# Part of one weight tile loaded through Pool's queue, in loads of uneven row counts

## The chip, the core and the metric

The kernel runs on one core of a Trainium2 chip. The core has a matrix engine (PE), a vector engine (DVE), a scalar engine (ACT), Pool (GpSimd) and the sync engine (SP), and 16 DMA engines that carry all transfers between HBM and the on-chip memory of 128 partitions. SP, ACT and Pool can each issue transfers, on a queue of their own; all queues run on the same 16 DMA engines. The metric is the device time of one execution in microseconds; smaller is better.

## The reference

One decoding step of a transformer block for 8 sequences, model width 512, in float32:

```python
mod = (silu(c) @ w_mod).reshape(8, 6, 1, 512)       # sa, ca, ga, sb, cb, gb
h = layernorm(x) * (1 + ca) + sa
q = (h @ wq) as 32 heads of 128;  k, v = last 2048 rows of the caches, 8 heads, each used by 4 query heads
p = softmax(q k^T / sqrt(128));  x = x + ga * ((p v) @ wo)
h = layernorm(x) * (1 + cb) + sb
x = x + gb * (relu(h @ w1 + b1) ** 2 @ w2 + b2)
```

The caches are 8 x 8 x 8192 x 128; the window of 2048 rows makes 67 MB of K and 67 MB of V. The weights are wq (512 x 4096), wo (4096 x 512), w_mod (512 x 3072), w1 (512 x 1792) and w2 (1792 x 512). Every byte is read once and little is computed on it.

## The kernel before

The kernel is a stream of loads with the computation hung on it. On chip stand four "big" slots of 128 partitions x 32 KB and one "small" slot of 128 x 16 KB. The list `loads` gives the order: w_mod in two parts, wq in two halves, then K and V tiles of 4 MB in turn (a K tile is half of the batch for one head; V runs two tiles behind K), with wo tiles of 2 MB slipped in before the K tiles 4, 9 and 13 into the small slot, and at the end the last V tile in three pieces, the "tail" (the last wo rows with half of w1), the other half of w1, and w2 in five pieces. `pump()` issues loads from this list in order as long as the slot that the next one needs is free; `done(key)` frees a slot and pumps again. All of them are issued by SP (`nc.sync`), so a load that waits for its slot also holds those behind it. ACT issues only the small xc at the start and the two biases b1, b2 near the end. Pool sets a few constants at the start and clears one tile (L498) near the end.

A wo tile j holds the wo rows of heads 2j and 2j+1, read as 128 partitions x 2 halves x 2048 floats (four consecutive wo rows for each partition and half, so each half is one run of 8 KB). The user is `project_o(hk)` (L482), which multiplies the attention output of head hk with half of the tile and adds into `wo_ps`; `done(("wo", j))` follows the second half. So the second wo tile (key `("wo", 1)`, issued before K tile 9) can be loaded once `project_o(1)` has read the first one, and is used by `project_o(2)` and `project_o(3)`. The last wo rows come with the tail, into a big slot, and are used by `project_o(6)` and `project_o(7)`.

The order of work is written by hand (`tc.manual_schedule()`): the loop at L506 takes K tile s//2 in quarter steps. In each step DVE transposes K (L184), PE makes scores (L353), and PE multiplies the probabilities of earlier tiles with V (L442); the softmax of a head is spread over steps (L361 to L429), and `parts`, `gather` and `project_o` follow (L459 to L482). After the loop come the residual, the second layer norm, w1 (L605) and w2 (L624), and the output. `spin` (L560) is filler work of PE. Semaphores and waits between engines are set by the framework from what each instruction reads and writes; a load waits for what last used its destination.

How a load is cut is set by the shape of its access pattern. A 4 MB tile of 128 partitions becomes 128 packets of 32 KB, 8 on each DMA engine, and one mark of completion on each.

Of the kernel before, what the change touches and what calls it, by code (L numbers as in the profile page):

```python
# [8 lines left out]
F32 = mybir.dt.float32  # L9
# [4 lines left out]
EPS = 1e-5  # L14
BIG_SLOTS = 4
PV_LAG = 5

@with_exitstack
def tile_adaln_cached_attention_mlp(  # L20
# [14 lines left out]
    nc = tc.nc  # L35
    P = 128
    B, HKV, SK, DH = k_cache.shape
    D = wq.shape[0]
# [14 lines left out]
    consts = ctx.enter_context(tc.tile_pool(name="consts", bufs=1))  # L53
# [27 lines left out]
    }  # L81
    free = {size: list(range(len(ts))) for size, ts in slots.items()}
    held = {}
    r_kc = "(p kc) n -> p kc n"

    def size_of(key):
        return "small" if key[0] in ("wo", "w1") or key == ("mod", 1) else "big"

    def load(key):
        kind, i = key  # L90
        held[key] = free[size_of(key)].pop(0)
        t = slots[size_of(key)][held[key]]
        if kind in "KV":

            hk, c = divmod(i, 2)
            v = k_cache[4 * c : 4 * c + 4, hk] if kind == "K" else v_cache[c::2, hk]
            v = v[:, SK - W :, :].rearrange("u (p j) d -> p u (j d)", j=NJ)
            cuts = (0, big // 2, big * 3 // 4, big) if key == ("V", 2 * HKV - 1) else (0, big)
            for x, y in zip(cuts, cuts[1:]):
                nc.sync.dma_start(t[:, x:y], v[..., x:y])  # L100
            return

        def rows(o, v):
            n = v.shape[1] * v.shape[2]
            nc.sync.dma_start(t[:, o : o + n].rearrange("p (a n) -> p a n", n=v.shape[2]), v)

        def wo_rows(j):

            r = 2 * REP * DH
            return wo[j * r : (j + 1) * r, :].rearrange("(h p i) n -> p h (i n)", p=P, i=4)  # L110

        w1v = w1.rearrange(r_kc, p=P)
        if kind == "wo":
            rows(0, wo_rows(i))
        elif kind == "mod":

            v = w_mod.rearrange("(p kc) n -> p (kc n)", p=P)
            nc.sync.dma_start(t, v[:, big:] if i else v[:, :big])
        elif kind == "wq":

            nc.sync.dma_start(t, wq.rearrange("(p h a) n -> h p (a n)", p=P, h=2)[i])
        elif kind == "tail":
            for h in range(2):
                rows(h * 4 * D, wo_rows(HKV // 2 - 1)[:, h : h + 1])
            rows(big // 2, w1v[:, 0:2])
        elif kind == "w1":
            rows(0, w1v[:, 2:4])
        else:
            v = w2.rearrange("(p c) n -> p c n", p=P)
            for lo, hi in ((0, 8), (8, 10), (10, 12), (12, 13), (13, 14)):  # L130
                rows(D * lo, v[:, lo:hi])
# [14 lines left out]
    def pump():  # L146
        while at[0] < len(loads) and free[size_of(loads[at[0]])]:
            load(loads[at[0]])
            at[0] += 1
# [53 lines left out]
    lo = consts.tile([P, 1], F32, name="lo")  # L203
# [25 lines left out]
    h = work.tile([P, P], F32, name="h_sb", tag="one_h_sb", bufs=1)  # L229
# [6 lines left out]
    for k in (2, 3, 4):  # L236
        n = 1 << k
# [27 lines left out]
    for i, last in enumerate((16, 8)):  # L265
        at_ = 0
        while at_ < last:
            kc, m = divmod(16 * i + at_, 6)
            n = min(4 - m if m < 4 else 6 - m, last - at_)
# [235 lines left out]

    for s in range(N + PV_LAG + 1):  # L506
        g, i = divmod(s, C)
        q, h = divmod(s, 2)
        v = s - PV_LAG
        soft = 1 <= g <= HKV  # L510
# [160 lines left out]
```

## Time and profile before

| | |
|---|---|
| median of 3 runs | 394.42 us (394.18 to 394.96) |
| profiled execution | 394.1 us, span 392.3 us |
| granted clock of PE, mean | 0.891 |
| busy: PE, DVE, ACT, POOL | 254.9, 218.0, 46.2, 1.3 us |
| read from HBM | 164.67 MB, 420 GB/s over the span |
| DMA packets | 7829, of which 7728 on SP's queue (q1) |

Times in the profile are microseconds from the start of the span. "DMA share" is the mean busy share of the 16 DMA engines in a stretch; records can overlap a little, so it can exceed 1. q1 is SP's queue and q10 ACT's; q8 and q14 are marked "instruction": they bring in instructions of the engines (16 KB and mostly 8 KB a packet) and take their time on the same DMA engines. "PEld" is the weight load of PE.

### The profile page before, as it was taken

To read this page: it belongs to the slowest core of one execution; us is meant where nothing else is said; L and a number is where in the kernel's file an instruction comes from. 1 tells how busy PE (TensorE), PEld (TensorE's weight loads), DVE (VectorE), ACT (ScalarE), POOL (GpSimd) and SP (SyncE) were. 2 spreads that over 40 slices of the span, in tenths; PEclk is the share of its full clock that TensorE was granted. 3 is DMA by queue.
4 is the path that set the end of the run, shared out by engine and by line. 5 is a ranking of instruction groups with operands and counts; after the bars stand their busy time and mean duration, and the time that the engine had idled before them with its cause. 6 is when DMAs were issued, how large, how long until landed. Compare 5 with 4: busy or idle time off the path is not lost.

```text
span 392.3 us, 4679 instructions
## 1 busy us (share of the span) xinstructions
PE 254.9 (65%) x2006; PEld 78.9 (20%) x2006; DVE 218.0 (56%) x323; ACT 46.2 (12%) x89; POOL 1.3 (0%) x8
## 2 busy tenths in 40 slices
PE   0075768668228973797375927883775837994996
PEld 0021200112001321232021202220221211222433
DVE  1370399959056845783582817780766357845231
ACT  0120201410003100310031003000201003004010
POOL 0000000000000000000000000000000000000000
PEclk9997789998859996999699688999788969997899
DMA  8999999999999999999999999999999999999994
GB/s 329 426 435 439 441 438 428 431 426 403 451 428 428 426 431 431 433 434 430 428 423 434 434 436 434 426 431 428 404 449 428 429 432 434 429 419 416 424 428 173
DMA packets 7829, 165.04 MB, mean 421 GB/s; under 512 B 856, under 2 KB 1024, under 8 KB 1536
## 3 DMA queue, kind: packets, MB, share of 16 engines
q1 hardware_dynamic: 7728, 164.70, 98.2%
q8 instruction: 16, 0.26, 0.3%
q10 hardware_dynamic: 80, 0.04, 0.0%
q14 instruction: 5, 0.04, 0.0%
HBM read 164.67 MB, written 0.07 MB: 420 GB/s over the span
## 4 chain that ended last, share of the span: by engine, by line
DMA 69%; DVE 15%; PE 13%; issue 2%; ACT 1%; ACTq 0%; POOL 0%; DVEq 0%; POOLq 0%; SPq 0%
DMA big<-in_A_k_cache_dram 55%; DVE kT L184 9%; PE s_ps L353 7%; DMA big<-in_A_wo_dram 6%; DMA big<-in_B_w_dram 5%; DMA xc_in<-in_xc_dram 3%; PE o_ps L442 2%; PE m_ps L298 1%; DVE pT L421 1%; PE p_ps L386 1%; DVE pr L414 1%; DVE o_sb L460 1%; DVE qst L262 0%; DVE o_sb L459 0%; ACT L227 0%
## 5 line engine op out<-in xcount | busy, mean ns | idle before, releaser
L184 DVE STREAM_TRANSPOSE kT<-big 128x1024 f32<-128x1024 f32 x128 | 151.5, 1221 | 91.4 <-DMA big<-in_A_k_cache_dram 87.8
L353 PE MATMUL s_ps<-kT,qst 128*32 128x512 f32 x512 | 129.8, 1074 | 21.3 <-DVE kT L184 21.1
L442 PE MATMUL o_ps<-big,pT 128*32 128x256 f32 x1024 | 71.3, 402 | 2.6 <-DMA big<-in_A_v_cache_dram 1.6
L442 PEld LDWEIGHTS o_ps<-big,pT 128*32 128x32 f32 x1024 | 34.3, 118 | 84.7 <-issue 66.6
L369 PE MATMUL m_ps<-ident,mx 128*1 128x128 f32 x16 | 4.3, 364 | 59.9 <-DVE mx L367 59.9
L353 PEld LDWEIGHTS s_ps<-kT,qst 128*32 128x32 f32 x512 | 16.0, 117 | 40.1 <-DVE kT L184 30.7
L421 DVE STREAM_TRANSPOSE pT<-pr 128x2048 f32<-128x2048 f32 x8 | 18.2, 2275 | 1.0 <-ACT pr L404 1.0
L404 ACT ACTIVATE pr<-pr,own 128x512 f32<-128x512 f32 x16 | 17.8, 1228 | 0.3
L363 ACT COPY ss<-s_ps 128x512 f32<-128x512 f32 x8 | 4.7, 586 | 101.7 <-issue 73.2
L398 ACT ACTIVATE pr<-p_ps,nm 128x512 f32<-128x512 f32 x8 | 5.5, 688 | 94.6 <-DVE nm L395 94.6
L341 ACT COPY qst<-q_ps 32x128 f32<-32x128 f32 x32 | 8.2, 257 | 71.2 <-PE q_ps L330 70.9
L298 PE MATMUL m_ps<-big,h1T 128*32 128x512 f32 x64 | 11.6, 896 | 6.1 <-DMA big<-in_A_wq_dram 4.1
L466 PE MATMUL m_ps<-o_sb,pick 128*128 128x256 f32 x16 | 6.2, 469 | 14.4 <-DVE o_sb L460 14.4
L369 PEld LDWEIGHTS m_ps<-ident,mx 128*1 128x1 f32 x16 | 0.7, 80 | 65.1 <-DVE mx L367 65.1
L218 PE MATMUL m_ps<-xsum,sel 128*128 128x1 f32 x2 | 0.6, 363 | 18.5 <-DVE xsum L216 18.5
L316 DVE COPY qbd<-m_ps 32x128 f32<-32x128 f32 x8 | 3.0, 373 | 16.3 <-PE m_ps L313 16.2
L386 PE MATMUL p_ps<-ss,perm 128*128 128x512 f32 x16 | 11.3, 792 | 0.0
L395 DVE COPY nm<-m_ps 128x1 f32<-128x1 f32 x8 | 1.3, 159 | 17.5 <-PE m_ps L391 17.5
L414 DVE TENSOR_SCALAR pr<-pr,own 128x512 f32<-128x512 f32 x16 | 9.2, 659 | 0.8 <-ACT pr L398 0.8
L459 DVE TENSOR_SCALAR o_sb<-o_ps,bit 128x128 f32<-128x128 f32 x16 | 4.9, 307 | 7.5 <-PE o_ps L442 7.5
L425 PE MATMUL m_ps<-zs,tsel 128*128 128x8 f32 x16 | 2.9, 252 | 9.0 <-DVE zs L416 9.0
L466 PEld LDWEIGHTS m_ps<-o_sb,pick 128*128 128x128 f32 x16 | 2.6, 203 | 25.9 <-DVE o_sb L460 25.9
(125 smaller groups left out, 118.4 us busy)
## 6 DMA issues: line engine op xcount, KB each, us to landing
big<-in_A_k_cache_dram SPq DMA_DIRECT2D x16, 4096.0 KB, 28.0
big<-in_A_v_cache_dram SPq DMA_DIRECT2D x15, 4096.0 KB, 20.4
big<-in_A_wq_dram SPq DMA_DIRECT2D x2, 4096.0 KB, 31.4
small<-in_A_wo_dram SPq DMA_DIRECT2D x3, 2048.0 KB, 34.0
big<-in_w_mod_dram SPq DMA_DIRECT2D x1, 4096.0 KB, 12.5
small<-in_w_mod_dram SPq DMA_DIRECT2D x1, 2048.0 KB, 16.9
big<-in_A_v_cache_dram SPq DMA_DIRECT2D x1, 2048.0 KB
big<-in_A_v_cache_dram SPq DMA_DIRECT2D x2, 1024.0 KB, 21.3
```

What stands on the lines that cost most here:

```text
L184: nc.vector.transpose(KTS[q, j][:, rows], k[:, rows, 32 * j : 32 * j + 32])
L298: nc.tensor.matmul(pqs[r][32 * g : 32 * g + 32, :], hT[:, kc, :], w[:, 4 * r + g, :], start=(kc == 0), stop=(kc == NQ - 1),)
L341: nc.scalar.copy(own[b, :, :, i, 0], pq[b, :P].rearrange("p (c m t) -> p c m t", c=2, t=REP))
L353: nc.tensor.matmul(s_ps[0][32 * g : 32 * g + 32, :], qst[hk % 2][:, P * (4 * c + u) + 32 * j :][:, :32], kT[:, u], start=(c == 0 and j == ...
L369: nc.tensor.matmul(MX_[hk][0:1, :P], mx, ident, start=True, stop=True)
L386: nc.tensor.matmul(sp, perm, SS_.pop(hk), start=True, stop=True)
L398: nc.scalar.activation(pr.rearrange("p j x -> p (j x)"), SS_.pop(hk), AF.Exp, bias=nm, scale=SCALE, accum_out=z)
L404: nc.scalar.mul(X_[hk][..., w], pr, own[:, w : w + 1])
L414: nc.vector.tensor_scalar(X_[hk][..., w], pr, own[:, w : w + 1], None, op0=ALU.mult)
L421: nc.vector.transpose(PT_[hk].rearrange("p e j r -> p j e r"), X_.pop(hk).rearrange("p j x w -> p j (x w)"))
L442: nc.tensor.matmul(O_[n][32 * g : 32 * g + 32, : 2 * DH], PT_[hk][:, e, j : j + 2].rearrange("p j r -> p (j r)"), vt[:, j : j + 2, :].rear ...
L466: nc.tensor.matmul(pp[:, : 2 * DH], pick.rearrange("p t u -> p (t u)"), o.rearrange("p e d -> p (e d)"), start=True, stop=True)
```

## The change

The second wo tile is no longer loaded by one SP transfer. SP loads the first 1536 of 2048 columns of each half row. Then Pool resets the cursor from which its queue deals transfers to DMA engines, and issues eight loads as `SHARES` lists them: those marked 1 load the last 512 columns (2 KB for each partition and half) of 19, 38, 19, 51 and 1 partitions, together all 128; those marked 0 load 4, 2 and 6 partitions x 2 x 4 floats into a tile `step` that nobody reads. Second, the last wo rows in the tail are loaded by one transfer instead of two of half the size. The computation is the same.

On the engines, Pool gets the reset and the eight loads, in front of its clearing of the tile of L498. The first dummy load waits for nothing, so it is issued at the start; the first real one waits for PE's L482 that last read the small slot; the second and third dummy load each wait for the dummy load before, because they write the same rows of `step`. PE's first use of the tile waits for Pool's five loads as well as for SP's, and so does SP's load of the third wo tile. SP issues as many loads as before up to the tail, and one less after that.

```diff
+LEFT = 1536
+SHARES = ((4, 0), (19, 1), (2, 0), (38, 1), (6, 0), (19, 1), (51, 1), (1, 1))
...
+    step = consts.tile([8, 2, 4], F32, name="step")
...
-        if kind == "wo":
+        if kind == "wo" and i == 1:
+
+            v = wo_rows(i)
+            d = t[:, : v.shape[1] * v.shape[2]].rearrange("p (a n) -> p a n", n=v.shape[2])
+            nc.sync.dma_start(d[:, :, :LEFT], v[:, :, :LEFT])
+            nc.gpsimd.inc_swdge_sem([], [], mode="reset_dge_cursor")
+            lo = 0
+            for n, real in SHARES:
+                if real:
+                    nc.gpsimd.dma_start(d[lo : lo + n, :, LEFT:], v[lo : lo + n, :, LEFT:])
+                    lo += n
+                else:
+                    nc.gpsimd.dma_start(step[:n], v[:n, :, :4])
+            assert lo == P
+        elif kind == "wo":
             rows(0, wo_rows(i))
...
         elif kind == "tail":
-            for h in range(2):
-                rows(h * 4 * D, wo_rows(HKV // 2 - 1)[:, h : h + 1])
+            rows(0, wo_rows(HKV // 2 - 1))
             rows(big // 2, w1v[:, 0:2])
```

## The prediction

> **What bounds the kernel now.** I read the page first (parts 2 to 4), then the chain of waits at its end, then the end in short stretches, because the change only moves DMA work from some of the 16 DMA engines to others.
>
> ```profile
> span 392.3 us, 4679 instructions
> DMA  8999999999999999999999999999999999999994
> q1 hardware_dynamic: 7728, 164.70, 98.2%
> q8 instruction: 16, 0.26, 0.3%
> DMA 69%; DVE 15%; PE 13%; issue 2%; ACT 1%; ACTq 0%; POOL 0%; DVEq 0%; POOLq 0%; SPq 0%
> ```
>
> The DMA engines are busy in every slice but the first and last, almost all of it SP's queue (q1). The run lasts as long as the bytes need. The chain of waits ends accordingly:
>
> ```profile
> 345.82 23.03 DMA big<-in_A_wo_dram
> 368.91 19.68 DMA big<-in_B_w_dram
> 388.59 0.04 issue
> 388.64 0.47 PE m_ps L624 x8
> 389.13 0.30 DVE y L632
> 389.46 0.29 DVE y L633
> ```
>
> The last piece of w2 lands at 388.59, and 3.7 us of fixed work follow. So the question is when the last of the 16 engines finishes its share. The view by stretches tells how many still work (columns: stretch, its length, PE, PEld, DVE, ACT, POOL, clock, DMA share, GB/s):
>
> ```profile
> 384.50:385.00 0.50, 0.50 (x2) 0.00 (x0) 0.00 (x0) 0.00 (x0) 0.00 (x0) 1.00 1.02 397
> 385.00:385.25 0.25, 0.25 (x9) 0.22 (x12) 0.00 (x0) 0.00 (x0) 0.00 (x0) 1.00 0.78 303
> 385.25:385.50 0.25, 0.25 (x17) 0.25 (x13) 0.00 (x0) 0.00 (x0) 0.00 (x0) 1.00 0.73 287
> 385.50:385.75 0.25, 0.25 (x20) 0.25 (x15) 0.00 (x0) 0.00 (x0) 0.00 (x0) 1.00 0.65 254
> 385.75:386.00 0.25, 0.25 (x20) 0.25 (x12) 0.00 (x0) 0.00 (x0) 0.00 (x0) 1.00 0.61 246
> 386.00:386.25 0.25, 0.25 (x17) 0.25 (x12) 0.00 (x0) 0.00 (x0) 0.00 (x0) 1.00 0.60 246
> 386.25:386.50 0.25, 0.25 (x20) 0.25 (x16) 0.00 (x0) 0.00 (x0) 0.00 (x0) 1.00 0.48 197
> 386.50:387.00 0.50, 0.50 (x28) 0.50 (x20) 0.00 (x0) 0.00 (x0) 0.00 (x0) 1.00 0.49 188
> 387.00:387.50 0.50, 0.50 (x23) 0.31 (x19) 0.00 (x0) 0.00 (x0) 0.00 (x0) 1.00 0.51 197
> 387.50:388.00 0.50, 0.49 (x16) 0.22 (x9) 0.00 (x0) 0.00 (x0) 0.00 (x0) 1.00 0.49 188
> 388.00:388.25 0.25, 0.25 (x8) 0.16 (x8) 0.00 (x0) 0.00 (x0) 0.00 (x0) 1.00 0.10 33
> ```
>
> Share times 16 is the number of busy engines: all until 385.0, about 12 until 385.5, 10 until 386.25, 8 until 388.0, none soon after. One half is done between 384.9 and 386.3, the other half only at 388.1. What is left after 385.0 is 0.25 x (0.78+0.73+0.65+0.61+0.60+0.48+0.10) + 0.5 x (0.49+0.51+0.49) = 1.73 us for each of the 16 engines, so evenly spread it would end at 386.73. Balancing can give 388.1 - 386.73 = 1.4 us at most.
>
> The late half is explained by instruction fetches, which run on the same engines. One 16 KB fetch of queue q8, and one 8 KB fetch of q14, in stretches of 4 us and 1 us:
>
> ```profile
> q8 instruction: 1, 0.02, 1.7%
> q14 instruction: 1, 0.01, 2.0%
> ```
>
> That is 1.7% of 64 engine-us, 1.09 us, and 2.0% of 16, 0.32 us, in which the one engine moves no data. Sixteen q8 fetches fall on few enough engines that half of them end two fetches behind. The views name no engine, so which these are has to be taken from the change's own numbers; I take it that they are those it spares. The second row, of 360.5 to 361.5, comes close to the end, and I return to it.
>
> **The change, part by part.** (1) The split of the second wo tile. SP now loads columns 0 to 1535 of each half row, and Pool's queue the last 512, in loads of 19, 38, 19, 51 and 1 rows, with three loads of 4, 2 and 6 rows of a dummy tile between them. What a row costs, from the rate of one engine:
>
> ```profile
> 362.00:370.00 8.00, 8.00 (x128) 4.10 (x120) 0.90 (x3) 0.00 (x0) 0.00 (x0) 0.80 1.02 422
> 386.50:387.50 1.00, 1.00 (x43) 0.81 (x35) 0.00 (x0) 0.00 (x0) 0.00 (x0) 1.00 0.50 193
> ```
>
> In pieces of 8 KB (first row, the wo tail among them) an engine moves 422 / (16 x 1.02) = 25.9 GB/s, in pieces of 4 and 2 KB (second row) 193 / (16 x 0.50) = 24.1. Of a whole tile each engine has 8 rows, whose last quarter is 16 pieces of 2 KB, 32.8 KB: 1.27 us that every engine is spared. An engine that gets 19 rows instead (77.8 KB) pays 3.23 us, net +1.96; one with 17 rows, a third of 51, 2.89 us, net +1.62; one with 1 row about -1.1.
>
> How many engines a load of n rows uses is seen in the trace only for small n. ACT's loads of xc and of the biases:
>
> ```profile
> q10 hardware_dynamic: 64, 0.03, 0.4%
> q10 hardware_dynamic: 16, 0.01, 1.1%
> ```
>
> Four loads of 8 rows made 64 packets, two loads of 4 rows made 16: a data packet for each row and one mark of completion with it, so n engines for n rows. For 19, 38 and 51 no row decides. I take the largest number up to 16 that divides them, 1, 2 and 3 engines, because n engines for n = 4, 2 and 6 and then 1, 2, 1, 3 walk once around 16 (4+1+2+2+6+1 = 16, then 3): seven engines are loaded, nine spared (one of these with the last row). [...]
>
> The sum: the late half ends at 388.1 - 1.27 = 386.8. Of the early half, those done by 385.5 end at 387.1 to 387.5 under +1.62 to +1.96. But the 0.60 against 0.48 shows two that work until 386.3. Seven loaded among eight early means that at least one of the two is loaded: it ends between 386.3 + 1.62 = 387.9 and 386.3 + 1.96 = 388.3, against 388.1 now. The 8 KB fetch at 361 is what made it late, I think: an engine that fetches little, hit once just before the end. So the bounds are -1.2 us (the straggler isn't loaded, or is not late this time) and +0.2; I take -0.3, nearer to the straggler's end since it stands in the rows.
>
> (2) Pool's issue. Pool does nothing between its setup and 359.58, so its own instructions delay nobody:
>
> ```profile
> 359.58 0.47 POOL L498 MEMSET pr<- 128x448 f32 x1 [358.14 <-DVE pT L421]
> 169.92 1.06 PE L482 MATMUL wo_ps<-small,oT 128*32 128x512 f32 x8
> 208.63 1.06 PE L482 MATMUL wo_ps<-small,oT 128*32 128x512 f32 x8
> 178.79 0.59 SPq L105 DMA_DIRECT2D small<-in_A_wo_dram  x1
> ```
>
> The first dummy load has nothing to wait for and goes at the start. The first real one waits for the release of the tile by L482 at 171.0, some 8 us ahead of SP's part; the dummies of 2 and 6 rows each wait for the dummy before, and hold up the loads behind them by a transfer. The user is L482 at 208.63: 37 us for 0.5 MB. If that cover went, PE would stop there, with L442 behind it and V's slots behind that. Pool's loads overtake SP's queue, so K and V between 171 and 204 land up to 3.2 us later on the loaded engines until SP's shortened part gives 1.27 us back. SP's loads are issued 20 to 28 us before they land (page, part 6), which hides that. SP's third wo load gains five waits, all long fulfilled; PE gains the same five at its L482 of 208.63. A few 0.05 us, hidden under DMA.
>
> (3) Marks. Each Pool load needs its completion told. Seven loads after 171: if only the engines used tell it, nothing. If all 16 do, each engine is visited seven times. Nearest rows: q10's 16 packets above took 1.1% of 48 engine-us, 0.033 us each, so 0.2 us in all at the q10 price, and 7 x 0.32 = 2.2 us at the price of the q14 fetch. I take 0.1 us, since a mark is the smaller of q10's two kinds of packet. [...]
>
> (4) The last wo rows in one load instead of two. SP issues one DMA less. Both halves now count as landed when the second did: 368.85 (345.82 + 23.03 above) plus 1.05 MB / 422 GB/s = 371.3. The user:
>
> ```profile
> 371.86 1.92 PE L482 MATMUL wo_ps<-big,oT 128*32 128x512 f32 x16
> 385.03 2.12 PEld L624 LDWEIGHTS m_ps<-big,pr 128*32 128x32 f32 x80 [0.76 <-issue]
> 382.26 2.84 PE L560 MATMUL q_ps<-ident 128*128 128x512 f32 x6
> ```
>
> L482 starts 0.5 us later than that, so nothing is lost; without this cover it would be the difference. The mark it saves is 0.03 us.
>
> What is late next, once DMA ends sooner: PE reaches L624 at 385.03, behind L560. At 2.12 / 80 = 26.5 ns each its 112 passes end at 388.0, against 389.1 now. So compute allows 1.1 us, more if the last K (whose landing DVE awaits) also lands sooner.
>
> Sum: -0.3 (split) - 0.03 + 0.1 (marks) = about -0.25 us. The profiled run took 394.1 us (span 392.3, 1.8 around it), 0.3 under the median of 394.42. From the median: 394.2.
>
> **The rivals.** *Even ends*: no straggler among the loaded engines. Then the end is 387.1 to 387.5 instead of 388.1, 0.6 to 1.0 us, with the compute bound just reached: 393.5. For it: the shares fit an 8/8 split closely. Against it: the two engines of 386.3.
>
> *Slower: marks or small pieces cost more on Pool's path.* If a visit costs each engine 0.32 us, as a q14 fetch does, the seven make +2.2 - 0.3 = +1.9 us: 396.3. The same comes of 38 pieces that each cost 0.05 us above SP's price. It decides from 0.16 us a visit. Against it: q10's 0.033 us. [...]
>
> *The split isn't what it seems*: each Pool load is spread over the engines, 19 rows as 2 each, 38 as 3, 51 as 4. Then the first engines get 2+3+2+4 = 11 rows (45 KB, 1.87 us, net +0.6) and the last three none. If late ones are among the first, the end moves to 388.7: 395.0. [...]
>
> **How the numbers follow.** A measurement of this kernel tells about 0.2%, 0.8 us, from no change. Forecast (straggler loaded, -0.8 to +0.2): 0.47, all of it within. Even ends: 0.29, of which 0.27 by over 0.2% (its range 393.2 to 393.8). Marks or pieces dearer: 0.16, of which 0.15 slower by over 0.2%. Spread otherwise or without effect: 0.08, of which 0.03 slower. Faster 0.27, within 0.55, slower 0.18. The range goes from 393.2 (even ends with all that compute allows) to 395.3, which covers the spread of 395.0 and leaves out the larger part of the dear marks. The forecast alone: 393.6 to 394.6.
>
> **What would show it.** Right: the DMA share at the end stays near 1 until after 386.5 and then falls within 1 us; w2 lands at 388.3; Pool's issues begin at about 171 and land before 190. Wrong: the share shows a plateau of a few engines (a straggler larger or smaller than I think), the landing of w2 after 389 (marks, small pieces), a wait of PE at L482 for Pool's loads, or a stretch in which the DMA share falls under 0.95 between 171 and 384.

## The result, and the profile after

The changed kernel takes 411.8 us (median of 6 runs, 411.35 to 412.6) against 394.3 us (394.11 to 395.1) for the kernel before: a ratio of 1.044, 95% interval 1.0426 to 1.0455. It is 17.5 us slower, where 394.2 us was predicted.

From here on line numbers are those of the kernel that is spoken of. In the changed kernel `project_o` is L498 (L482 before), the dummy loads are L128, Pool's other loads L125, SP's part of the tile L120, SP's loads of K and V L103 and DVE's transposes of K L200. First the page of the profile of the changed kernel: two rows of its 40 slices, the queues, and a group of instructions.

```profile
DMA  9999999999999999999999906999999999999995
GB/s 357 414 436 430 425 441 412 454 414 433 435 422 441 414 451 417 435 424 410 374 401 425 358 11 257 432 436 419 451 414 448 414 451 416 430 437 405 419 431 208
...
q1 hardware_dynamic: 7712, 164.17, 94.5%
q0 software_dynamic: 1376, 0.53, 0.6%
...
L498 PE MATMUL wo_ps<-small,oT 128*32 128x512 f32 x48 | 8.2, 619 | 28.1 <-DMA small<-in_A_wo_dram 28.1
```

The DMA engines, 0.99 busy before, stand still in one slice of 10 us (share 0, 11 GB/s). Pool's queue q0 needed 0.6% of the DMA time, so its bytes cost next to nothing. And PE waits 28.1 us at `project_o`, for a load of the small slot. The chain of work that ended last, of the changed kernel (start, duration, what), tells how this came about:

```profile
171.24 1.03 POOL small L125
172.27 29.93 DMA step<-in_A_wo_dram
202.20 0.29 issue
202.49 0.59 POOL step L128
203.07 1.99 POOL small L125 x2
205.06 33.96 DMA small<-in_A_wo_dram
239.02 0.14 issue
239.16 0.64 PE wo_ps L498
...
250.62 19.98 DMA big<-in_A_k_cache_dram
```

A dummy load of 64 bytes takes 29.93 us, and the loads of 19, 51 and 1 rows issued behind it take another 33.96. That is the longest part of the way from the release of the slot at 171 to 239. The DMA issues between 160 and 260 us (issuing queue, count, KB of one, median time from issue to landing) show that all five loads of the tile by Pool were so slow (30.5 to 39.0 us; the one of 204 KB took 34.8), and SP's much larger ones were not:

```profile
big<-in_A_k_cache_dram SPq DMA_DIRECT2D x4, 4096.0 KB, 21.3
...
small<-in_A_wo_dram POOLq DMA_DIRECT2D x2, 76.0 KB, 32.4
small<-in_A_wo_dram POOLq DMA_DIRECT2D x1, 152.0 KB, 39.0
...
small<-in_A_wo_dram POOLq DMA_DIRECT2D x1, 4.0 KB, 34.0
```

What the stop sets off is seen in the timeline of SP's queue and in the stretches, of the changed kernel and then of the kernel before:

```profile
207.83 0.53 SPq L103 DMA_DIRECT2D big<-in_A_k_cache_dram  x1
248.44 0.54 SPq L103 DMA_DIRECT2D big<-in_A_v_cache_dram  x1
```

```profile
200.00:220.00 20.00, 8.44 (x66) 2.11 (x54) 11.50 (x16) 2.36 (x4) 3.12 (x4) 0.87 1.02 400
220.00:240.00 20.00, 0.84 (x8) 0.44 (x12) 1.42 (x2) 0.00 (x0) 0.00 (x0) 0.50 0.77 307
240.00:260.00 20.00, 19.40 (x151) 5.85 (x147) 12.03 (x15) 2.39 (x7) 0.00 (x0) 0.95 0.52 212
...
239.00:248.00 9.00, 8.85 (x68) 3.00 (x71) 2.79 (x3) 1.03 (x4) 0.00 (x0) 0.82 0.00 0
```

```profile
200.00:220.00 20.00, 11.66 (x97) 3.69 (x90) 12.64 (x18) 2.03 (x6) 0.00 (x0) 0.87 1.03 439
220.00:240.00 20.00, 11.62 (x88) 3.25 (x80) 9.76 (x13) 0.59 (x1) 0.00 (x0) 0.78 1.01 432
240.00:260.00 20.00, 16.64 (x137) 5.09 (x140) 16.07 (x20) 4.05 (x8) 0.00 (x0) 1.00 1.01 432
```

(The columns are PE, PEld, DVE, ACT and POOL busy, the granted clock, the DMA share, and GB/s.) PE stops, so it releases no K or V slot; SP issues nothing between 207.83 and 248.44; and when the tiles in flight have landed, the DMA engines stand still, from 239 to 248 altogether. The share lost is (1.01 - 0.77) x 20 + (1.01 - 0.52) x 20 = 14.6 us. The rest of the 17.5 us is another kind of loss: between 200 and 220 the engines are busy as before, 1.02 of the time, and yet move 400 GB/s instead of 439; between 170 and 200 they move 411 instead of 423. At 432 GB/s these two make 1.8 and 0.8 us.

So there are two questions. Why do small loads take 30 us? And why does a busy engine move less?

### The profile page after: what moved, and what is told of

It reads as the page before. It is cut to its first block, busy times and chain, and to the rows that moved or that the text cites. A ratio compares the mean times of both kernels' runs of the same rounds, so it can differ in the third digit from the quotient of the medians.

```text
span 409.9 us, 4695 instructions
## 1 busy us (share of the span) xinstructions
PE 254.9 (62%) x2006; PEld 77.7 (19%) x2006; DVE 218.0 (53%) x323; ACT 46.2 (11%) x89; POOL 7.8 (2%) x16
## 3 DMA queue, kind: packets, MB, share of 16 engines
q0 software_dynamic: 1376, 0.53, 0.6%
## 4 chain that ended last, share of the span: by engine, by line
DMA 64%; PE 15%; DVE 14%; issue 3%; ACT 2%; POOL 1%; ACTq 0%; DVEq 0%; POOLq 0%
DMA big<-in_A_k_cache_dram 41%; DMA small<-in_A_wo_dram 8%; DMA step<-in_A_wo_dram 7%; DVE kT L200 7%; PE s_ps L369 6%; DMA big<-in_B_w_dram 5%; PE o_ps L458 4%; DMA xc_in<-in_xc_dram 3%; DVE pT L437 2%; PE p_ps L402 1%; PE m_ps L314 1%; POOL small L125 1%; DVE pr L430 1%; DVE mx L383 1%; PE wo_ps L498 0%
## 5 line engine op out<-in xcount | busy, mean ns | idle before, releaser
L200 DVE STREAM_TRANSPOSE kT<-big 128x1024 f32<-128x1024 f32 x128 | 151.5, 1220 | 108.1 <-DMA big<-in_A_k_cache_dram 82.3
L498 PE MATMUL wo_ps<-small,oT 128*32 128x512 f32 x48 | 8.2, 619 | 28.1 <-DMA small<-in_A_wo_dram 28.1
L482 PE MATMUL m_ps<-o_sb,pick 128*128 128x256 f32 x16 | 6.1, 466 | 14.4 <-DVE o_sb L476 14.4
L498 PEld LDWEIGHTS wo_ps<-small,oT 128*32 128x32 f32 x48 | 1.9, 129 | 38.0 <-issue 33.5
## 6 DMA issues: line engine op xcount, KB each, us to landing
big<-in_w_mod_dram SPq DMA_DIRECT2D x1, 4096.0 KB, 12.7
```

Of the source, the lines that this page charges most:

```text
L200: nc.vector.transpose(KTS[q, j][:, rows], k[:, rows, 32 * j : 32 * j + 32])
L482: nc.tensor.matmul(pp[:, : 2 * DH], pick.rearrange("p t u -> p (t u)"), o.rearrange("p e d -> p (e d)"), start=True, stop=True)
L498: nc.tensor.matmul(wo_ps[32 * i : 32 * i + 32, :], oT[hk % 2][:, i, :], w[:, 4 * (hk % 2) + i, :], start=(hk == 0), stop=(hk == HKV - 1),)
```

## The experiments: why Pool's loads take so long

Theory A, the queue: on each DMA engine, packets of Pool's queue and of SP's queue are taken in turn, so a packet of Pool waits for one of SP, 32 KB or 1.22 us, however small it is itself. What counts is the number of packets that a load puts on an engine. The rivals, B and W in the expectations, lay it to the waits of the dummy loads, each of which holds up Pool's loads behind it.

**Own tiles for the dummies.** Each dummy load has a tile of its own, so none waits for another.

```diff
-    step = consts.tile([8, 2, 4], F32, name="step")
+    steps = [consts.tile([8, 2, 4], F32, name=f"step{i}") for i in range(len(SHARES))]
...
-            for n, real in SHARES:
+            for (n, real), step in zip(SHARES, steps):
```

> The changed kernel, but each dummy load writes a tile of its own, so no dummy waits for the one before and Pool issues all its loads from 171 us on. Theory A (each DMA engine alternates packet by packet between Pool's queue and SP's, so every packet of Pool costs one 32 KB packet of SP, 1.2 us, and each Pool load puts about 9 packets on every engine): the number of packets is what it was, so Pool's last load still lands near 230 to 238 us and the time stays at 407 to 412 us. Theory B (a Pool load lands behind all that SP had queued when it was issued, about 29 us): all land by 178 + 30 = 208, PE does not stop, 394 to 396 us. Theory W (the two waits of the dummies alone are the fault): as B.

Measured: 412.02 us, ratio to the kernel before 1.0446 (1.0425 to 1.0467), as the change itself. The timeline of Pool and the waits of PE in this kernel:

```profile
174.94 0.59 POOL L128 DMA_DIRECT2D step<-in_A_wo_dram  x1
175.52 2.54 POOL L125 DMA_DIRECT2D small<-in_A_wo_dram  x3
```

```profile
PE wo_ps L498 <- DMA small<-in_A_wo_dram: 27.0, 1, 27.0
```

The last loads are issued at 175.5 instead of 203.1, 27.5 us earlier, and PE waits 27.0 us instead of 28.1. The waits of the dummies cost nothing: Pool's queue was full of work in any case. The rivals fall.

**One load by Pool.** The same last quarter of the tile, in one load of 128 rows.

```diff
-SHARES = ((4, 0), (19, 1), (2, 0), (38, 1), (6, 0), (19, 1), (51, 1), (1, 1))
+SHARES = ((128, 1),)
```

> The changed kernel, but the last quarter goes in one Pool load of all 128 rows, with no dummies and no uneven shares. Theory A: 8 data packets and about 9 others on each engine, 17 to 18 times 1.2 us: lands 21 us after its issue, near 192 us, no stop of PE; 394.4 us, within 0.2% of before. Theory B: lands after about 29 us, near 200; also 394.4 us. If Pool's path is slow in itself, it lands later than 208 and the time rises by what it is late.

Measured: 394.42 us, ratio 0.9996 (0.9983 to 1.0009), and no wait of PE for it. From the page and the DMA issues of this kernel:

```profile
q0 software_dynamic: 144, 0.52, 0.3%
```

```profile
small<-in_A_wo_dram POOLq DMA_DIRECT2D x1, 512.0 KB, 16.9
```

144 packets are 9 for each engine, eight rows and a mark. The same bytes in the change were 1376 packets, 86 for each engine. This number can be worked out: if a load puts on every engine as many packets as its busiest engine has rows, and a mark, the eight loads of 4, 19, 2, 38, 6, 19, 51 and 1 rows make 1 + 19 + 1 + 19 + 1 + 19 + 17 + 1 = 78 and 8 marks, 86 and 16 x 86 = 1376. The packet records agree in detail: 127 packets of 4 KB and two of 2 KB are the 128 rows, 8 and 4 of the dummies' rows have 32 bytes (4 in the first load, which goes at the start), and 1093 of 8 bytes fill the other engines up. So 19 rows on one engine are 19 turns on all sixteen. The turns themselves stand in the trace of the changed kernel: between 178 and 200 us, with both queues at work, Pool's queue has 364 packets and SP's 362, and SP's packets of 32 KB took 1.25 us in the mean from 171 to 203 us (1.22 in the kernel before). The count of 1376 also confirms that 38 rows go to two engines and 51 to three. These are the numbers of engines that the prediction took, the largest up to 16 that divides the rows (the divisor rule of the expectations below). Spread as in its rival, 19 rows as 2 each, 38 as 3 and 51 as 4, the eight loads would have made 15 packets and 8 marks an engine, 23 and not 86; the four cheap loads below were spread. The 364 against 362 agree with packets taken in turn, as theory A has it. The turns fit the 29.93 us of the first dummy wait: ahead of it and with it stand 19 + 1 + 1 + 1 = 22 packets, by 1.25 us 27.5 us; the 2.4 us that remain are put down to a start and weren't measured by themselves.

**Smaller packets of SP.** The K tiles 7 to 11 and V tiles 5 to 10 are loaded in two halves, so that SP's packets beside Pool's have 16 KB.

```diff
+            if (kind == "K" and 7 <= i <= 11) or (kind == "V" and 5 <= i <= 10):
+                cuts = (0, big // 2, big)
```

> The changed kernel, but SP loads the K tiles 7 to 11 and the V tiles 5 to 10 in two halves each, in packets of 16 KB (0.61 us) instead of 32 KB (1.2 us); as many bytes stand in SP's queue. Theory A: Pool's packets wait half as long: the dummy of 2 rows lands about 15 us after its issue instead of 30, the last loads come in by about 205 to 212, and the time falls to 394 to 399 us. Theory B: the bytes queued ahead are the same, so the dummy still takes about 30 us and the time stays at 410 to 412 us.

Measured: 400.99 us, ratio 1.0167 (1.0146 to 1.0187). The timeline of Pool, of the changed kernel and then of this one (the bracket is Pool's idle time before the line and what ended it):

```profile
202.49 0.59 POOL L128 DMA_DIRECT2D step<-in_A_wo_dram  x1 [28.63 <-DMA step<-in_A_wo_dram]
```

```profile
191.97 0.59 POOL L130 DMA_DIRECT2D step<-in_A_wo_dram  x1 [18.07 <-DMA step<-in_A_wo_dram]
```

Nothing was changed in Pool's loads, and the dummy's wait went from 28.63 to 18.07 us: 22 turns of 0.63 us (half of 1.25) are 13.8, and some 4 us are left for the start. PE's wait at `project_o` went from 28.1 to 13.8 us. The size of the *other* queue's packets sets the time, as the turns would have it and theory B would not. The forecast of A was still too good: 394 to 399 us with the last loads in by 212, where they came in at about 225.

**Sixteens.** All loads by Pool have a multiple of 16 rows, so none leaves an engine with filler; eight loads, three of them dummies, as in the change.

```diff
-SHARES = ((4, 0), (19, 1), (2, 0), (38, 1), (6, 0), (19, 1), (51, 1), (1, 1))
+SHARES = ((16, 0), (16, 1), (16, 0), (32, 1), (16, 0), (16, 1), (48, 1), (16, 1))
```

> The changed kernel with eight Pool loads as before, but all of row counts that 16 divides: dummies of 16 rows, real loads of 16, 32, 16, 48 and 16, so every DMA engine gets the same. Theory P (a Pool load puts on every engine as many packets as its busiest engine has rows, the others filled with packets of 8 bytes; each packet waits for one of SP's and costs about 0.06 us): 19 packets on each engine instead of 86, so Pool's loads land before 208, PE does not stop, and the cost is about 1 us: 394.5 to 395.5. Theory M (a fixed cost of each Pool load, 4.9 / 8 = 0.6 us, however many packets): 399, as with the uneven loads of the first wo tile.

Measured: 398.04 us, ratio 1.0092 (1.0072 to 1.0112). There are 304 packets, 19 an engine; PE no longer waits. Pool's wait for the dummy, by the timeline of this kernel:

```profile
181.67 0.50 POOL L128 DMA_DIRECT2D step<-in_A_wo_dram  x1 [9.19 <-DMA step<-in_A_wo_dram]
```

Four turns of 1.25 us are 5, and some 4 us are again left for the start. So the stop of PE is gone with the filler, but 3.6 us remain. The forecast for few packets, 394.5 to 395.5, was missed. That is the second question.

**The first wo tile instead of the second.** The change's own loads, applied to the tile that is used later after its release: Pool issues them from 27.95 us on, and the tile's first use is at 138 us, so they have 110 us.

```diff
-        if kind == "wo" and i == 1:
+        if kind == "wo" and i == 0:
```

> The changed kernel with the same shares, but taken from the first wo tile instead of the second: its slot is free from about 13 us and its first use is at about 130 us, so Pool's loads have 115 us instead of 37. Theories A and B: they land by 60 to 110 us, PE does not stop, and what is left is the evening out of the DMA engines: 0.3 us faster than before by the prediction's sum (one straggler), up to 1.0 if the ends are even; 393.4 to 394.1 us. If marks or small pieces cost more than reckoned: 395 or more.

Measured: 399.28 us, ratio 1.0123 (1.0108 to 1.0138), and PE doesn't wait for it. So 4.8 us are lost without PE's stop. If the loads cost the same in both places, the stop was 12.7 of the 17.5 us; the change's own stretches gave 14.6, and the difference isn't accounted for. The 4.8 us are lost where Pool's loads run, as the stretches show, of the kernel before and of this one:

```profile
20.00:60.00 40.00, 28.62 (x172) 7.08 (x172) 21.27 (x48) 4.11 (x10) 0.00 (x0) 0.83 1.00 428
60.00:100.00 40.00, 30.65 (x196) 6.96 (x196) 31.23 (x34) 6.92 (x14) 0.00 (x0) 0.96 0.99 425
100.00:140.00 40.00, 23.41 (x188) 7.13 (x184) 23.18 (x29) 4.63 (x9) 0.00 (x0) 0.83 1.01 432
```

```profile
20.00:60.00 40.00, 27.81 (x172) 7.09 (x172) 19.66 (x46) 4.32 (x11) 2.61 (x3) 0.83 1.00 417
60.00:100.00 40.00, 27.51 (x158) 6.04 (x157) 30.26 (x32) 6.89 (x14) 3.13 (x4) 0.83 1.00 409
100.00:140.00 40.00, 21.85 (x170) 6.29 (x162) 19.92 (x28) 3.60 (x5) 0.00 (x0) 0.79 1.01 401
...
391.00:392.00 1.00, 1.00 (x46) 1.00 (x39) 0.00 (x0) 0.00 (x0) 0.00 (x0) 1.00 0.92 354
392.00:393.00 1.00, 0.94 (x31) 0.41 (x23) 0.00 (x0) 0.00 (x0) 0.00 (x0) 1.00 0.48 182
```

The share stays at 1.00 to 1.01, the rate falls by 11, 16 and 31 GB/s: 58 x 40 / 430 = 5.4 us. The last two rows are the end of the run. Before, half the engines worked on alone for 2 us (share 0.50 in the prediction's row from 386.5); here the share is still 0.92 until 392, 1.5 us before the last piece lands. The end is evened out as the change meant it, and the sixteen marks with which the last piece of w2 lands, as many as there are engines, say how much that is worth:

```
last piece of w2 landed, us      first   mean    last    last - mean
kernel before                    385.33  387.17  388.59  1.42
changed kernel                   404.61  405.47  406.28  0.81
first wo tile                    391.10  392.85  393.52  0.67
sixteens (nothing evened out)    388.94  390.85  392.33  1.48
```

0.6 to 0.75 us gained at the end; in the first-tile run for a mean that is 5.7 us later.

## The experiments: why a busy engine moves less

**Cheap loads at the start.** The kernel before, with small loads into tiles that nobody reads, issued in the first microseconds: four by Pool of 19 rows x 16 bytes, nine by Pool of 128 rows x 16 bytes, and the same nine by ACT.

```diff
+    for i in range(4):                                  # then: range(9)
+        junk = consts.tile([19, 4], F32, name=f"junk{i}")    # then: [128, 4]
+        nc.gpsimd.dma_start(junk, wo[:19, :4])               # then: wo[:128, :4]; by ACT: nc.scalar
```

> The kernel before, with nothing changed but four Pool loads of 19 rows x 16 bytes into tiles that nobody reads, issued at the start. Theory P: 4 x (19 + 1) = 80 packets on each engine at 0.06 us, 4.8 us: 399.2. Theory M: 4 x 0.6 = 2.4 us: 396.8. If what the first wo tile's run lost came of the 2 KB pieces or of the uneven shares, not of packets: 394.4.

> The kernel before and nine Pool loads of 128 rows x 16 bytes into tiles that nobody reads, issued at the start: 81 packets on each engine, none of them filling. If any packet of Pool's queue costs 0.06 us beside SP's 32 KB packets: 399.2. If only the 8-byte filling does: 394.5 to 395. Theory M: 9 x 0.6 = 5.4 us, 399.8.

> As the run with nine even Pool loads, but ACT issues them on its queue. If any second queue costs SP's queue 0.06 us a packet: 399. If it is Pool's queue alone: 394.5 to 395.5, with ACT's nine issues early in the run hidden under the loads.

Measured, in this order: 395.06 us, ratio 1.0008 (0.9997 to 1.0019); 395.96 us, 1.0041 (1.0027 to 1.0054); 398.66 us, 1.0107 (1.0082 to 1.0132). The first two didn't test what they were meant to, because Pool's queue put several rows of 16 bytes into a packet: 128 packets in all for the four loads, 288 of up to 128 bytes for the nine. The four loads show something else. By the packet records they made 36 packets of 32 bytes, 4 of 20 and 24 of 8, beside 64 marks: for each load two rows on each of nine engines, one on a tenth and filler on six. So these 19 rows were spread over the engines, 2 each, as in the prediction's rival, while the 19 rows of the change went to one. What decides between the two ways wasn't tested. On ACT's queue the rows stayed apart, 1152 packets of 16 bytes. But there SP's second load was issued at 13.99 us instead of 1.18, while ACT issued its nine loads (2.83 to 16.51), and the DMA share from 9 to 15 us was 0.57 (0.90 before). So most of this run's 4.2 us is SP issuing late, not packets in turn; why SP was held isn't shown. All that follows is that loads of a few KB cost from nothing that can be measured to 4.2 us.

**Eight loads of 16 rows, neighbours or strided; four of 32.** The last quarter by Pool without dummies: in eight loads of 16 neighbouring partitions, in eight loads of every eighth partition, and in four loads of every fourth.

```diff
-            for n, real in SHARES:
-                ...
+            for m in range(8):          # neighbours
+                nc.gpsimd.dma_start(d[16 * m : 16 * m + 16, :, LEFT:], v[16 * m : 16 * m + 16, :, LEFT:])
...
+            for m in range(8):          # strided; and with 4 in place of 8 the four loads
+                nc.gpsimd.dma_start(d[m::8, :, LEFT:], v[m::8, :, LEFT:])
```

> The last quarter of the second wo tile goes by Pool in eight loads of 16 neighbouring partitions each, without dummy loads. It holds 256 pieces of 2 KB and eight marks, 24 packets for each DMA engine, about as many as the one load of 128 rows, which cost nothing (ratio 0.9996). Theory P (what costs is the number of Pool loads, or that a load's 16 pieces go into 16 neighbouring partitions): as the sixteens, where SP's packets slowed to 1.39 us between 180 and 200, so about 398 us, ratio 1.009. Rival Q (the loss there came of the dummies and their waits): 394.4, ratio 1.000. No wait of PE for Pool's loads, which land by about 200.

> The same eight loads of 16 partitions, but each takes every eighth partition. Number of loads, packets and bytes are those of the load of neighbours. If the number of loads (their marks, their start) is what costs, the time is the same as there, about 398 us. If it is that 16 engines write into 16 neighbouring partitions at once, the cost goes: 394.4 to 395, ratio 1.000 to 1.002.

> The last quarter by Pool in four loads of 32 strided partitions: the 128 pieces and bytes of the eight strided loads (ratio 1.0084), with half as many loads and marks. If each Pool load costs every DMA engine a fixed time (3.0 us / 8 = 0.37 us), 394.45 + 4 x 0.37 = 395.9, ratio 1.004. If the cost comes only of loads that give an engine a single row, 394.5, ratio 1.000.

Measured: neighbours 398.48 us, ratio 1.0102 (1.0088 to 1.0116); strided 397.43, 1.0084 (1.0069 to 1.0099); four strided 394.19, 0.9998 (0.9989 to 1.0008). The stretch from 175 to 195 us of the kernel before, of the four, of the eight strided and of the eight neighbours:

```profile
175.00:195.00 20.00, 10.74 (x94) 3.07 (x83) 10.09 (x13) 0.59 (x1) 0.00 (x0) 0.83 1.01 434
```

```profile
175.00:195.00 20.00, 9.01 (x86) 2.93 (x81) 8.37 (x10) 0.59 (x1) 0.00 (x0) 0.80 1.02 433
```

```profile
175.00:195.00 20.00, 8.87 (x88) 2.65 (x76) 7.04 (x9) 0.59 (x1) 0.27 (x1) 0.89 1.01 382
```

```profile
175.00:195.00 20.00, 9.67 (x84) 2.84 (x76) 5.53 (x7) 0.58 (x1) 0.22 (x1) 0.80 1.03 354
```

The same bytes in the same time move at 434, 433, 382 and 354 GB/s, all with busy engines. After the first two of these runs a fixed price of a Pool load seemed the better theory (strided cost nearly what neighbours did). The four loads refute it: they should have cost 1.5 us and cost nothing. They don't refute that a load costs when it gives each engine a single row; they were two rows on each (192 packets, 12 an engine, against 256, 16 an engine, for the eight).

**The tail alone.** The kernel before, with only the second part of the change.

```diff
-            for h in range(2):
-                rows(h * 4 * D, wo_rows(HKV // 2 - 1)[:, h : h + 1])
+            rows(0, wo_rows(HKV // 2 - 1))
```

> Only the second part of the change: the last wo rows in one load instead of two. One DMA less on SP's queue and one mark less on each engine (0.03 us); the first user of these rows starts no later than now. 394.4 us, ratio 0.999 to 1.001. If it cost anything of the 17.5 us that the change lost, the ratio would be over 1.002.

Measured: 394.2 us, ratio 0.9999 (0.9991 to 1.0008). This part costs and gains nothing.

**The evening-out by SP's queue, and by two Pool loads.** In the first, SP loads 1920 of 2048 columns and then the rest in loads of 57, 69 and 2 rows; in the second, Pool loads 102 and 26 rows after one dummy of 15 rows at the start.

```diff
-LEFT = 1536
+LEFT = 1920
...
+            for n in (57, 69, 2):
+                nc.sync.dma_start(d[lo : lo + n, :, LEFT:], v[lo : lo + n, :, LEFT:])
+                lo += n
```

```diff
-SHARES = ((4, 0), (19, 1), (2, 0), (38, 1), (6, 0), (19, 1), (51, 1), (1, 1))
+SHARES = ((15, 0), (102, 1), (26, 1))
```

> The evening-out without Pool's queue: SP loads 1920 of 2048 columns of the second wo tile, and then the last 128 columns (1 KB a partition in two pieces of 512 bytes) in loads of 57, 69 and 2 rows, which by the divisor rule go to 3, 3 and 2 engines from the first on; the tail's last wo rows in one load. If SP's queue deals from the first engine on in each load, the other engines are spared 8 rows of 1 KB, 8.2 KB or 0.32 us, so the end comes up to 0.32 us earlier: 394.1, ratio 0.999, hardly to be told from 1. If uneven loads cost SP's own packets as Pool's do, 395 or more. Nothing waits for it: the tile lands before 204, its use is at 208.6.

> The evening-out with fewer loads: one dummy load of 15 rows at the start, then 102 rows (by the divisor rule 17 on each of six engines) and 26 rows (2 on each of thirteen), and the tail in one load. The engines that bring in PE's instructions get 2 rows of 4 KB instead of 8 and are spared 24.6 KB, 0.95 us. Packets on each engine after the release: 17 + 1 + 2 + 1 = 21, by the alternation with packets of 1.25 us about 26 us and a start of some 4 us: landed at about 201, no stop of PE at 208. Gain of even ends 0.4 to 0.9 us, cost of two Pool loads 0.7 to 1.4 us, so 394.3 to 395.4; faster than before (393.9) only if the loads' cost is at its low end.

Measured: by SP 395.35 us, ratio 1.0026 (1.0018 to 1.0035), a loss where a gain of 0.3 us was expected if uneven loads were free; no view shows to how many engines SP's three loads went. By two Pool loads 399.56 us, 1.0128 (1.0113 to 1.0143), against 394.3 to 395.4 expected. PE doesn't stop in either; the second lost 5.4 us with two loads. Its stretch from 170 to 200 us:

```profile
170.00:200.00 30.00, 15.48 (x132) 5.17 (x124) 14.53 (x17) 1.61 (x5) 1.56 (x2) 0.77 1.01 381
```

381 GB/s against 423 before, at a share of 1.01. By the packet records SP's packets of 32 KB beside these loads (176 to 198 us) took 1.42 us in the mean instead of 1.22, and as long behind 8-byte filler as behind rows. So neither the number of loads nor the engine's own work decides.

**By ACT.** The eight strided loads, issued by ACT.

```diff
-                nc.gpsimd.dma_start(d[m::8, :, LEFT:], v[m::8, :, LEFT:])
+                nc.scalar.dma_start(d[m::8, :, LEFT:], v[m::8, :, LEFT:])
```

> The eight strided loads of 16 partitions, issued by ACT instead of Pool (ACT idles from 173.4 to 183.6 there in the trace of before). If the cost belongs to Pool's path, it goes: 394.5, ratio 1.000. If it belongs to small loads beside SP's packets on any queue: 397 to 398, ratio 1.007 to 1.009. Some packets are split differently on this queue (two of 2 KB for a partition instead of one of 4 KB), which alone would add 8 turns an engine and little time.

Measured: 399.1 us, ratio 1.0116 (1.01 to 1.0131), above both forecasts. Most of this loss is of another kind. The stretch from 176 to 183, and SP's issues one after the other:

```profile
176.00:183.00 7.00, 5.74 (x52) 1.61 (x48) 4.10 (x5) 0.00 (x0) 0.00 (x0) 1.00 0.58 181
```

```profile
162.05 0.54 SPq L103 DMA_DIRECT2D big<-in_A_v_cache_dram  x1
181.58 0.54 SPq L103 DMA_DIRECT2D big<-in_A_k_cache_dram  x1
```

The engines are idle for 42% of 7 us, 2.9 us, because SP issued nothing for 19 us: the K tile that goes out at 181.58 went out at 167.75 in the kernel before. ACT issued its eight loads from 172.96 to 181.90, so SP's gap began before them. The profile puts SP's wait, 18.9 us, down to a DMA into the small slot; why a K tile should wait for that is open. At 181 GB/s instead of 430, this stretch alone loses 4.1 of the 4.9 us, and from 183 to 200 the rate is 432. So this run doesn't tell whether the slowing of busy engines needs Pool's queue. The K tiles below do.

**A K tile in eight loads.** The kernel before, with K tile 9 in eight loads on SP's own queue, in three ways. In the first, each load's outer axis has four rows only and the rows come to other partitions than they should (the scores of this tile are of other keys). In the second, load m brings partitions m, m+8, m+16 and so on. The third loads the same rows as the second into the 16 neighbours from 16m (again other keys' scores). The amount of work is the same in all.

```diff
+            if key == ("K", 9):
+                for m in range(8):
+                    u, h = m % 4, m // 4
+                    nc.sync.dma_start(t[m::8], v[m::8])                        # first
+                    nc.sync.dma_start(t[m::8], v[h::2, u])                     # second
+                    nc.sync.dma_start(t[16 * m : 16 * m + 16], v[h::2, u])     # third
+                return
```

> The kernel before, but its K tile 9 in eight loads of 16 strided partitions on SP's own queue: the same 128 packets of 32 KB, with seven marks more on each engine. If a load with one row an engine slows the next packet on whatever queue (in the evening-out by SP the packets of 32 KB behind the small loads took 1.69 us in place of 1.22), 7 x 0.3 to 0.47 = 2 to 3.3 us: 396.5 to 397.7, ratio 1.005 to 1.008. If marks and loads are free on SP's queue: 394.5, ratio 1.000.

> The kernel before, with K tile 9 in eight loads on SP's queue, load m bringing partitions m, m+8, m+16 and so on: 16 rows of 32 KB, one for each engine, and if row j goes to engine j each engine writes only into the eight partitions 8j to 8j+7 that it writes in whole tiles too. Theory G (what slows the packets is that several engines write into the same group of partitions): 394.2 plus seven marks, ratio 1.000 to 1.001. Theory L (a load that gives an engine one packet and one mark costs time whatever it writes): 2 to 3 us, ratio 1.005 to 1.008.

> The same eight loads from the same rows of K, but load m goes to the 16 neighbouring partitions 16m to 16m+15 (so K's rows of this tile stand in other partitions, and the scores of this tile are those of other keys; the amount of work is the same). Theory G: 16 engines write into two groups of eight partitions at a time; the packets of 32 KB take a multiple of 1.22 us, and the run is 10 us or more longer than with rows of the own group. Theory L: the same time as that run.

Measured: 440.5 us, ratio 1.1172 (1.1153 to 1.119); 405.96 us, 1.0287 (1.0272 to 1.0302); 415.32 us, 1.0527 (1.0506 to 1.0547). The first is an error of the edit: with four rows on the outer axis each load went to four engines, to judge by the rate (it fell to 105 GB/s, four times 26, for some 20 us), so it doesn't answer its question. The other two read the same rows and differ only in the partitions that are written, and neither uses Pool's queue. So 9.4 us between them come of where a load writes. Their stretches, strided and then neighbours, beside 423 GB/s in the kernel before:

```profile
215.00:225.00 10.00, 0.00 (x0) 0.00 (x0) 0.00 (x0) 0.00 (x0) 0.00 (x0) 0.50 0.96 210
```

```profile
215.00:225.00 10.00, 0.00 (x0) 0.00 (x0) 0.00 (x0) 0.00 (x0) 0.00 (x0) 0.55 1.02 167
```

The packets of 32 KB took 2.5 us (strided) and 3.4 us (neighbours) in place of 1.22, by the packet records, and an instruction fetch of 16 KB on one of the engines 1.36 and 1.60 us in place of 1.07. Each of both theories is refuted as I had put it: rows at a distance of eight weren't free (G with groups of eight neighbours), and the partitions do matter (L).

What is left is that the partitions matter, and in both pairs in the same direction:

```
load                                       measured
4 MB tile, or Pool's 128 rows              428 to 434 GB/s, loss 0
Pool, 32 rows, every fourth partition      433, loss 0
Pool, 16 rows, every eighth partition      382, loss 3.0 us
Pool, 16 neighbouring rows                 354, loss 4.0 us
K, 16 rows, every eighth partition         210
K, 16 neighbouring rows                    167
```

Sixteen neighbouring rows move less than 16 rows of every eighth partition (354 against 382 GB/s, 167 against 210), and 32 rows of every fourth partition move as much as a whole tile. The reason wasn't shown: no view tells which engine writes which partitions. Nor was the place told apart from the single row: all loads of this table under 428 GB/s give an engine one row and then a mark, and loads of 16 rows that lie in another way weren't run. That the strided K tile is slower than the whole tile could also come of that, or of the order in which K is read. The single row can't be all, since the two uneven loads lost 5.4 us with 17 rows on an engine. Whether the loss of the uneven loads, in the change, by two Pool loads and by SP, comes of where they write wasn't shown.

## Why the prediction was wrong, point by point

**The step that failed** is part (2), Pool's issue, in two sentences: the dummies "hold up the loads behind them by a transfer", and "The user is L482 at 208.63: 37 us for 0.5 MB." Neither sentence has a time for such a transfer; the bound that they led to, landed before 190, leaves 19 us for all of Pool's loads. On a queue that stood beside a saturated one, a load's time was its packets per engine times the other queue's packet: 84 packets after 171 us (the 86 less the two of the dummy at the start), with 37 / 1.25 = 30 turns to be had. Not every turn was so dear, or the 84 would have taken 105 us and not 68: sixteen for each engine stood beside SP's pieces of 6 KB (0.29 us), and the last ones beside a queue that had run empty. The cover held for one load (16.9 us), for the sixteens and for two uneven loads; for these loads it was too short by about 30 us. The bound "landed before 190" was thus wrong by 49 us. What came of it is what the prediction named if the cover went, PE's stop, V's slots behind it, and then the DMA's; it was given as a condition and had no chance of its own. In "What would show it" both signs stood: a wait of PE at `project_o` for Pool's loads, and a share under 0.95 before 384.

**Part (1), the split.** The mechanism fits. The loads went to 1, 2, 1 and 3 engines, by the count of 1376 packets, and the end evened out by 0.6 to 0.75 us; that the relieved engines were those made late by PE's fetches can't be seen, since no view names an engine. This is the rival "Even ends" (0.6 to 1.0); the straggler, for which I took -0.3, didn't show: the last piece in the first-tile run landed at 393.52, with the ones before it at 393.5 and 393.3. What the step left out is the other engines. "An engine that gets 19 rows instead (77.8 KB) pays 3.23 us" priced an engine by its own rate, and nothing for the others; but in the first-tile run the rate of all engines together fell by 11 to 31 GB/s at a full share. That the others paid because of where the rows were written would be an estimate from the K tiles (9.4 us between two ways of writing the same rows); it wasn't shown.

**Part (3), marks and pieces.** I took 0.1 us, and +2.2 as the price of the rival on the slow side ("marks or small pieces cost more on Pool's path", 396.3). The side was right, the reason not: the four strided loads have four marks and pieces as small, and lost nothing. The first-tile run lost 4.8 us net, 5.4 us by its rates. So even without the stop the kernel would have come out at about 399, above the range, if the loads cost the same in both places.

**Part (4), the tail in one load**: right, 0.9999 (0.9991 to 1.0008).

**The rivals.** *Spread over the engines* is refuted for the change by the 86 packets, though the four cheap loads were spread. No effect, the other case in the 0.08, fell too: 411.8 us against 394.3, and the queue mattered by its turns (364 packets against 362). None of the rivals had PE's stop, though half of the number for it could be had from the profile before: a 4 MB tile is 8 packets on each engine and takes 4.19 MB / 432 GB/s = 9.7 us, so a turn is 1.2 us, and 37 us are 30 turns. The other half, the filler that makes the 84 packets, stood in no row of it.

What stays open: how much of the first-tile run's 5.4 us comes of where the rows are written and how much of the turns themselves; the two are in every uneven load together. That SP issued late in both runs with many loads on ACT's queue was seen and not explained.

## What to carry to other kernels

Beside SP's queue, when it keeps the DMA engines full with packets of 32 KB, count a load of Pool's queue in turns: rows on its busiest engine plus one mark, each for 1.25 us, and this for every engine (22 turns were 27.5 of the 29.93 us of a 64-byte load). Load all 128 partitions at once: 16 rows at a time cost 3 to 4 us here where the same bytes in one load, or in four of every fourth partition, cost nothing. An imbalance of 1.4 us at the end wasn't worth a remedy that touches every engine's stream: the evening-out gained 0.6 to 0.75 us in the two forms in which that was measured, and all four forms tried lost.

## What the runs showed of the hardware that was not expected

- Engines without a share in an uneven Pool load of this tile get 8-byte packets instead, up to as many as the busiest engine has rows: 1093 of the 1376 packets.
- Pool loads of 19 rows went to one engine when each row was two pieces of 2 KB (by the 86 packets an engine), and two rows to an engine when each row was one run of 16 bytes (36 packets of 32 bytes in four loads).
- The time of a 64-byte load followed the packets of the other queue: 29.9 us beside 32 KB, 19.4 us beside 16 KB.
- The DMA share didn't tell a slowed engine: 1.02 at 433 GB/s, 1.03 at 354 and 0.96 at 210. Share and rate have to be read together.
- Pool's queue merged rows of 16 bytes into packets of up to 128 bytes; ACT's queue sent 1152 single ones. So the queue, too, and not the access pattern alone, had a part in how a load was cut.
- In both runs with eight or nine loads on ACT's queue, SP's next load went out 13 to 14 us later than in the kernel before, and the DMA engines ran out of work.
